# Masks built on GpSimd, single score tiles issued in runs, and a rewritten order, in a one-core attention plus feed-forward kernel

## The chip, the cores and the metric

The kernel runs on one core of a Trainium2 chip. A core has five engines that run side by side and meet through semaphores: TensorE (PE in the profile; PEld is its weight load), VectorE (DVE), ScalarE (ACT), GpSimd (POOL) and SyncE (SP), which here issues most of the data transfers. The metric is the device time of one execution in microseconds; the kernel before takes 184.63 us as the median of three runs (184.52 to 184.64).

## The reference

Four batches, eight heads, 768 positions, head size 64. Heads marked in `is_retrieval` see all earlier positions; the others see the first 4 positions (the sinks) and the last 64. After the attention, the 512 columns of the heads go through a feed-forward layer with two up projections of 1024 columns, their maximum, and one down projection.

```python
scores = scale * np.matmul(q, k.transpose(0, 1, 3, 2))
full_mask   = causal                              # retrieval heads: 0, 2 and 6
stream_mask = causal & (is_sink | in_win)         # the other five heads
a = softmax(np.where(mask, scores, -1e9))
x = np.matmul(a, v) -> (batch*seq, heads*head_dim)
out = np.maximum(x @ w1, x @ w2) @ w_out
```

## The kernel before, in words

**Pieces of work.** A batch is cut into two halves of 384 query rows, written (b, hf). For each half the heads are taken in four pairs; at run time `head_order` finds which heads are full ones, and the pairs are "FF", "FS", "SS", "SS". A pair of a half goes through these steps: a load of q, k and v into `ld` (`load_half`, by SP); casts to bf16 into `qb` and `vb` (`cast_qk`, `cast_v`, any of DVE, ACT, POOL); a transpose on PE into a PSUM bank (`turn`, line 712); the copy back into `qk` (`unturn`); copies for the window heads (`mix_k`, `mix_v` into `kx`, `vx`). Then come the scores (`scores`, matmuls at line 893, on 64 rows each, two heads side by side), their exponentials (`exp`, ACT, line 912) into one of the `at` buffers, a multiplication with 0/1 masks (`mask`, DVE, line 931), the weighted sums (`weighted`, line 956), the division (`normalise`), and the transpose of x.

**Feed-forward.** The maximum is rewritten: max(x w1, x w2) = relu(x (w1 - w2)) + x w2. `prep_weights` makes `w12` = w1 - w2 in four column chunks (`sub`, DVE, line 1122), and `w2o` = w2 w_out out of transposes of w2 (line 1138) and matmuls (line 1156). `forward` then computes, for each half, eight blocks of x times `w12` (line 1177), the relu, and the output from both parts (line 1227), which is copied to `ot` and stored by SP (line 1244).

**Order.** Every step is an `Op` with estimated costs on the engines that could do it; `Order.run` walks through time, and by ranks (`RANK`), free PSUM banks, waits and margins gives each engine its list of instructions. PE has several lists (scores "S", weighted sums "W", feed-forward "F", turns "TQ" and so on) and takes the first list whose head can run. These are estimates used while the program is built; on the chip only the resulting order and its semaphores count. SP issues the loads in the order of `LOADS` and the ranks: q, k, the mask table and v of the first half, q and k of the second, w2, v of the second half, w1. The four pieces of w_out are loaded by POOL (line 616). Until 38 us of the plan, PE gets matmuls on a zero tile (`warmer`, line 471) where it has nothing else.

**Masks.** Identity and masks (1152 bf16 columns) are computed on the host and held in a table in DRAM. ACT issues the load of the identity (line 1558), SP the load of the other 1024 columns (`load_table`, line 595) as its third transfer. DVE turns four parts of them into 0/1 masks (`kept`, line 646). In the very first half the masks are instead added into the scores by matmuls (line 867).

**Score tiles.** `attend` makes one step out of two tiles of scores at a time (`TOGETHER`; in the first half one), each tile with two PSUM banks; six `at` buffers hold the exponentials (`NAT`).

**The end.** The last rows of the output are made in two parts of 256 columns; ACT copies each to `ot` and SP stores it. A check (`judge`, `say`) writes a verdict; every engine loads it (line 1569) and jumps (line 1572) over a second program, `tile_any_heads`, that is there for inputs with another set of heads and doesn't run here. The end of the program is a barrier of all engines.

Of the kernel before, what the change touches and what calls it, by code (L numbers as in the profile page):

```python
# [11 lines left out]
F32 = mybir.dt.float32  # L12
# [27 lines left out]
def one(p, hh, blocks):  # L40
# [96 lines left out]
class Order:  # L137
# [6 lines left out]
    def __init__(self, banks, dummy, dummies_until):  # L144
        self.ops, self.lists, self.n, self.shift = [], {}, 0, 0.0
        self.banks, self.freed = [None] * banks, [0.0] * banks
        self.at, self.dummy, self.dummies_until = {}, dummy, dummies_until
# [41 lines left out]

    def run(self, names, allowed):  # L190
# [11 lines left out]
        rings, served = {"SP": [], "POOL": []}, [0.0, 0]  # L202
# [16 lines left out]
        def begin(o, e, t):  # L219
            cost = o.costs[e]  # L220
# [53 lines left out]
        left = len(self.ops)  # L274
        while events:
# [25 lines left out]
            while again:  # L301
# [20 lines left out]
                for relaxed in (False, True):  # L322
                    chosen = None
                    for n in names:
# [10 lines left out]
                        if o.claims and self.place(o.claims, False, SPARE.get(n, 0)) is None:  # L335
                            continue
                        chosen = n, o
                        break
                    if chosen:
# [4 lines left out]
                        begin(o, "PE", t)  # L344
                        again = True
                        break
                else:
                    if t < self.dummies_until:
                        spot = self.place([("dummy", 1)], False)
                        last = 0.107 if t < COLD_UNTIL else 0.056  # L350
                        if spot and (t < COLD_UNTIL or used(t) < WARM_SHARE):
                            self.dummy(spot["dummy"][0])
                            done_pe.append((t, t + last, 1.0))
                        if spot:
                            free["PE"] = t + last
                            push(t + last, None)
# [7 lines left out]
REGISTERS = 4.4  # L364
TURNED_BY_PE = (0,)
# [3 lines left out]
    'cast': 3.05, 'vcast': 13.85, 'unturn': 4.05, 'mix_k': -0.7, 'mix_v': -14.35, 'exp': 4.1,  # L369
    'mask': -5.1, 'norm': -4.75, 'take_x': -8.75, 'turn': 8.65, 'w2b': 9.4, 'sub': -4.6, 'w2t':  # L370
    -8.95, 'wob': -4.45, 'w2o': -10.4, 'relu': -0.25, 'load': 10.7, 'out': -0.6, 'h2': 7.85,
    'table': -2.75, 'vload': -2.25,
# [5 lines left out]
NAT = 6  # L378
# [23 lines left out]
DMA_LATE = {'SP': 2.7, 'POOL': 3.2}  # L402
RING = 4224
SPLIT = ((0, 0),)
K_BY_ACT = False
K_LANDS = 7.6
# [4 lines left out]
RATE = {'first': 0.3, 'long': 0.34, 'v': 0.27, 'w': 0.36, 'wo': 0.37, 'cast': 0.22}  # L411
SPARE = {}
STEP = 2.4
FF_STEP = -2.1
S_AFTER = 2
PE_BEGINS = 1.0
# [3 lines left out]
MARGIN = {'W': 2.0, 'S': 0.8, 'F': 2.0, 'TQ': 0.8}  # L420
X_MARGIN = 1.5


def tile_three_full_heads(
    tc, q, k, v, w1, w2, wo, out, tab, table_dram, heads, rez, found, verdict, warm, early_k, lds
# [18 lines left out]
    NLD, NQB, NQK, NMIX, NAT, NX, NXT, NG, NOUT = 3, 4, 8, 6, 6, 2, 4, 2, 4  # L444
# [33 lines left out]
    def copy(e, out, in_):  # L478
        if e == "ACT":
            nc.scalar.copy(out=out, in_=in_)  # L480
        else:
            eng[e].tensor_copy(out=out, in_=in_)  # L482

# [3 lines left out]
    def act(n):  # L487
        return 0.065 + n / 1200
# [17 lines left out]
    def load_half(b, hf, kinds=(0, 1, 2)):  # L506
# [33 lines left out]
        if (b, hf) == (0, 0) and 0 in kinds:  # L540
            order_.insert(2 if long else 2 * NT, (3, 0))
        for t, i in order_:
# [3 lines left out]
            if t == 3:  # L546
                bias_in.append(load_table(128, 1152))
            elif t < 2 and long:
# [45 lines left out]
    def load_table(lo, hi):  # L594
        return dma(0.262, lambda _: nc.sync.dma_start(
            out=tab[:, lo:hi], in_=table_dram.ap()[:, lo:hi]
        ), rate=0.4, parts=128, grain=85.0)

# [25 lines left out]
    for what in LOADS:  # L624
        kind, c = what[:2], int(what[2:]) if what[:1] == "w" else 0
        if what[0] in "AB":
            kinds = (2,) if what[1:] else (0, 1)
            load_half(0, "AB".index(what[0]), kinds)
            flow += loads[0, "AB".index(what[0]), kinds[-1]]
# [6 lines left out]
    registers = order.given(REGISTERS)  # L636

# [143 lines left out]
    def prepare(b, hf, p):  # L781
# [7 lines left out]
        else:  # L789
# [4 lines left out]
            for hh in range(2):  # L794
                for lo, hi in ((0, 1), (1, 2)) if (b, hf) in SPLIT else ((0, 2),):
# [3 lines left out]
                        tag=f"cast{b}.{hf}.{p}", rank=RANK["cast"], port=("DVE", "POOL"),  # L799
# [814 lines left out]
```

## Time and profile before

| | |
|---|---|
| median of three runs | 184.63 us (184.52 to 184.64) |
| the profiled execution, its own time | 184.92 us |
| its span, first to last instruction | 182.0 us |
| what lies around the span (difference) | 2.92 us |
| busy: PE, DVE, ACT, POOL | 94%, 53%, 72%, 23% of the span |
| granted TensorE clock | 0.998 |

The profile has a page and a trace. On the page are the busy times of the engines, the span in 40 slices, the transfers, the chain of work that ended last (followed back from the end), and groups of instructions by source line. The trace answers further questions: a timeline of one engine in a stretch of time, the busy time in chosen stretches, and all instructions of one source line with their times, also those that only an engine's sequencer runs (a name such as ACTq). In a timeline a row is: start in us, length in us, engine, line, operation, output<-input, shapes, count, and in brackets the idle time before it with what ended it. Matmuls of one row overlap, so the start of the next row tells how long a group took.

### The profile page before, as it was taken

What the parts mean: (1) busy time and instruction counts of PE and PEld (TensorE: products, weight loads), DVE (VectorE), ACT (ScalarE), POOL (GpSimd) and SP (SyncE); (2) the same over time, 40 slices, a digit from 0 to 9 for tenths busy, and PEclk for the clock granted to TensorE, in tenths of its full rate; (3) what the DMA queues carried; (4) which work ended last, traced back from release to release, by engine and by line L of the source; (5) the groups of instructions that cost most, each with busy time, mean ns of one, the idle gap of its engine ahead of it and who ended that gap; (6) DMA issues with size and microseconds to landing.
All of it is one profiled execution on the core that took longest, in us unless ns stands there. A gap on an engine that the chain in (4) does not pass through costs nothing.

```text
span 182.0 us, 4932 instructions
## 1 busy us (share of the span) xinstructions
PE 171.5 (94%) x1836; PEld 105.3 (58%) x1836; DVE 96.7 (53%) x283; ACT 131.6 (72%) x287; POOL 42.4 (23%) x77
## 2 busy tenths in 40 slices
PE   7599599989999999999999999999999999999991
PEld 7567486466647656565545565565466545545560
DVE  3356896599689984576247476656447500000000
ACT  3399794596899999999996984777797524525430
POOL 1000810100609489899580000000000000000000
PEclk9999999999999999999999999999999999999999
DMA  4999999999899999999999994160151052012022
GB/s 136 323 242 339 347 223 244 349 290 280 221 290 270 326 294 295 160 243 202 179 140 147 248 177 118 63 144 0 61 144 61 0 144 115 11 58 115 0 99 87
DMA packets 74930, 32.68 MB, mean 180 GB/s; under 512 B 54162, under 2 KB 71826, under 8 KB 74898
## 3 DMA queue, kind: packets, MB, share of 16 engines
q1 hardware_dynamic: 54848, 28.84, 62.4%
q0 software_dynamic: 19904, 3.41, 25.4%
q8 instruction: 16, 0.26, 0.6%
q14 instruction: 16, 0.13, 0.2%
q10 hardware_dynamic: 146, 0.03, 0.1%
HBM read 25.46 MB, written 6.29 MB: 174 GB/s over the span
## 4 chain that ended last, share of the span: by engine, by line
PE 64%; SPq 11%; DMA 9%; DVE 5%; ACT 4%; issue 2%; POOL 2%; POOLq 0%; DVEq 0%; ACTq 0%
PE ps L1227 30%; PE ps L1177 20%; DMA ld<-in_v_dram 6%; PE ps L956 6%; PE ps L893 6%; SPq L523 5%; SPq L608 3%; DMA ld<-in_q_dram 3%; DVE w L1122 2%; SPq L513 2%; PE ps L712 2%; ACT at L912 2%; ACT qk L480 1%; POOL qb L482 1%; DVE at L931 1%
## 5 line engine op out<-in xcount | busy, mean ns | idle before, releaser
L912 ACT ACTIVATE at<-ps 128x512 bf16<-128x512 f32 (+2 forms) x134 | 65.1, 601 | 3.5 <-PE ps L893 1.9
L1227 PE MATMUL ps<-wob,g 128*128 128x512 bf16 (+1 forms) x200 | 46.8, 371 | 0.2 <-ACT at L912 0.2
L1177 PE MATMUL ps<-xt,w 128*128 128x384 bf16 x256 | 46.0, 326 | 0.9 <-DVE w L1122 0.7
L1177 PEld LDWEIGHTS <-w 128*128 128x128 bf16 x256 | 23.6, 97 | 15.9 <-issue 0.9
L931 DVE TENSOR_TENSOR at<-at,tab 128x1024 bf16<-128x1024 bf16 (+5 forms) x49 | 25.6, 538 | 13.3 <-ACT at L912 13.0
L1201 ACT ACTIVATE g<-ps 128x384 bf16<-128x384 f32 x56 | 27.5, 504 | 7.0 <-PE ps L1177 6.5
L1227 PEld LDWEIGHTS <-g 128*128 128x128 bf16 x200 | 18.2, 98 | 17.8 <-issue 0.4
L480 ACT COPY ot<-ps 128x512 f32<-128x512 f32 (+1 forms) x20 | 11.4, 572 | 22.8 <-PE ps L1227 22.6
L1227 PE MATMUL ps<-w2o,xt 128*128 128x512 bf16 (+1 forms) x100 | 24.8, 371 | 0.3 <-ACT qk L480 0.3
L956 PEld LDWEIGHTS <-at 128*128 128x128 bf16 x477 | 19.9, 97 | 7.3 <-issue 0.2
L983 DVE TENSOR_TENSOR x<-ps,rez 128x192 f32 x64 | 22.8, 356 | 1.8 <-DVE x L983 0.2
L956 PE MATMUL ps<-vb,at 128*128 128x65 bf16 x387 | 21.6, 193 | 0.0
L482 POOL CAST qb<-ld 128x384 bf16 x23 | 12.1, 561 | 35.6 <-DMA ld<-in_k_dram 35.6
L893 PE MATMUL ps<-qk 64*128 64x128 bf16 (+1 forms) x322 | 20.2, 230 | 0.0
L893 PEld LDWEIGHTS <-qk 64*128 64x128 bf16 x322 | 12.0, 94 | 11.2 <-issue 8.2
L1227 PEld LDWEIGHTS <-xt 128*128 128x128 bf16 x100 | 9.2, 98 | 9.0 <-issue 0.5
L712 PE MATMUL ps<-tab,qb 128*128 128x128 bf16 x144 | 10.4, 219 | 4.0 <-DVE qb L482 2.1
L480 ACT COPY qk<-ps 128x768 bf16<-128x768 bf16 x17 | 12.9, 816 | 0.6 <-PE ps L712 0.6
L480 ACT CAST qb<-ld 128x384 bf16 (+1 forms) x23 | 8.8, 453 | 6.1 <-DMA ld<-in_k_dram 3.7
L471 PE MATMUL ps<-warmer 128*128 128x128 bf16 x147 | 11.0, 236 | 1.1 <-POOL warmer L1552 1.1
L712 PEld LDWEIGHTS <-qb 128*128 128x128 bf16 x144 | 8.3, 98 | 5.0 <-ACT qb L480 2.3
L471 PEld LDWEIGHTS <-warmer 128*128 128x128 bf16 x147 | 9.8, 107 | 1.4 <-POOL warmer L1552 1.1
(62 smaller groups left out, 145.5 us busy)
## 6 DMA issues: line engine op xcount, KB each, us to landing
out_dram<-ot SPq DMA_DIRECT2D x23, 256.0 KB, 2.1
ld<-in_q_dram SPq DMA_DIRECT2D x6, 768.0 KB, 7.0
ld<-in_k_dram SPq DMA_DIRECT2D x6, 768.0 KB, 7.4
ld<-in_v_dram SPq DMA_DIRECT2D x18, 256.0 KB, 6.7
ld<-in_moe_w_dram SPq DMA_DIRECT2D x8, 512.0 KB, 8.2
wob<-in_moe_w_out_dram POOLq DMA_DIRECT2D x4, 256.0 KB, 8.1
ld<-in_q_dram POOLq DMA_DIRECT2D x8, 96.0 KB, 6.6
ld<-in_k_dram POOLq DMA_DIRECT2D x8, 96.0 KB, 6.7
```

The lines of the kernel that those rows point to most:

```text
L471: nc.tensor.matmul(banks[e][:, 0:128], lhsT=warm, rhs=warm, start=True, stop=True)
L480: nc.scalar.copy(out=out, in_=in_)
L482: eng[e].tensor_copy(out=out, in_=in_)
L712: nc.tensor.transpose(to[:, i], qbs[:, T["qb", n, hf] % NQB, t, i].rearrange("p h d -> p (h d)"), ident)
L893: nc.tensor.matmul(to.rearrange("p (i c) -> p i c", c=128), lhsT=lhsT, rhs=q_of(n, i, m)[rows], start=bk not in under, stop=True, skip_gro ...
L912: nc.scalar.activation(out=at[:, bk, 0:w], in_=bank(("ps", b, hf, t), part=bk)[:, 0:w], func=ACT.Exp, scale=scale,)
L931: eng[e].tensor_tensor(out=at, in0=at, in1=tbl, op=ALU.mult)
L956: nc.tensor.matmul(po[:, hh, i - NT * hf, :], lhsT=ats[:, T["at", b, hf, t] % NAT, bk, e * 128:(e + 1) * 128], rhs=rhs, start=first, stop= ...
L983: nc.vector.tensor_tensor(out=xs[:, (2 * b + hf) % NX, :, bass.ds(heads[2 * p + hh], 1), :], in0=po[:, hh, :, 0:D].unsqueeze(2), in1=z[:, ...
L1177: nc.tensor.matmul(bank(key)[:, 0:HALF], lhsT=w[:, kc, fc * 128:(fc + 1) * 128], rhs=xts[:, (2 * b + hf) % NXT, :, kc, :], start=(kc == 0) ...
L1201: nc.scalar.activation(out=g, in_=ph, func=ACT.Relu)
L1227: nc.tensor.matmul(bank(key)[:, cols], lhsT=lhsT, rhs=(w2o if kind == "x" else wob)[:, c, cols], start=(e == 0), stop=(e == len(steps) - 1),)
```

## The change

1. The masks and the identity are no longer loaded. DVE zeroes the table, and POOL writes it with eight `affine_select` instructions and two copies (`mask_table`). The planner is told that they are there at 6.5 us (`MASKS_MADE`). The built program has, on POOL, one library-reload instruction ahead of the first select.
2. Each tile of scores is a step of its own; `run_of_scores` lets PE begin with scores only if two (at the end of a half three) tiles can be issued one after the other, with their banks free. The planner charges for entering and leaving scores.
3. `at` has eight buffers in place of six; `ok` lies in `lds`, whose loads are over by then.
4. The two halves of the first batch have ranks of their own (`FRONT`, `rank_of`), all ranks, margins, biases and rates have new numbers, and `LOADS` has the weights in another order. So the order of instructions is new on each engine.
5. The last store is issued by ACT, which also makes the copy before it (`LAST_BY_ACT`).
6. `tile_any_heads`, which doesn't run, takes three tiles of scores per exponential: its part on ACT shrinks from 393 to 135 instructions; those of PE, DVE and POOL (9803, 3165, 256) stay.

```diff
-TOGETHER = (
-    [[0, 1], [2, 3], [4, 5], [6]], [[0, 1], [2, 3], [4, 5], [6, 7], [8, 9]],
-    [[0], [1], [2], [3], [4], [5]],
-)
...
+    def run_of_scores(self, first, t):
+        mine = self.lists["S"][first:]
+        mine = [o for o in mine if o.tag[1:3] == mine[0].tag[1:3]]
+        n = 1 if self.stuck or mine[0].tag[1:3] == (0, 0) else min(S_RUN, len(mine))
+        if len(mine) - n == 1 and not self.stuck:
+            n += S_REST
+        if any(o.left or o.ready > t + 1e-9 for o in mine[:n]):
+            return False
+        return sum(e is None for e in self.banks) >= 2 * n
...
-                    for n in names:
+                    for n in ("S", *names) if last == "S" else names:
...
+                        if n == "S" and last != "S" and not self.run_of_scores(at[n], t):
+                            continue
...
+                        extra = ENTER_S if n == "S" and last != "S" else LEAVE_S if last == "S" and n != "S" else 0.0
...
+MASKS_MADE = 6.5
-NAT = 6
+NAT = 8
-    'A', 'Av', 'B', 'w23', 'wo0', 'wo1', 'wo2', 'w20', 'wo3', 'w21', 'w11', 'w10', 'w12', 'w22',
+    'A', 'Av', 'B', 'wo1', 'w20', 'w21', 'wo0', 'wo2', 'w12', 'w10', 'w23', 'w22', 'wo3', 'w11',
     'w13', 'Bv',
-BIAS = {'DVE': 1, 'ACT': 0}
+BIAS = {'DVE': 2.5, 'ACT': 0}
+LAST_BY_ACT = True
+S_RUN = 2
+S_REST = 1
+ENTER_S = 0.1
+LEAVE_S = 0.11
-MARGIN = {'W': 2.0, 'S': 0.8, 'F': 2.0, 'TQ': 0.8}
+MARGIN = {'W': 0.3, 'S': 0.8, 'F': 2.0, 'TQ': 0}
+FRONT = (
+    {'mix_k': -2.8, 'mask': -4.7, 'unturn': -0.4, 'exp': -10.3, 'vcast': -3.0, 'cast': -3.8,
+    'norm': -0.3}, {'vcast': -1.7, 'unturn': -1.3, 'exp': 0.5, 'mask': -2.7, 'norm': 4.4,
+    'mix_k': 1.8, 'cast': -1.5},
+)
...
-        if (b, hf) == (0, 0) and 0 in kinds:
-            order_.insert(2 if long else 2 * NT, (3, 0))
-            if t == 3:
-                bias_in.append(load_table(128, 1152))
...
+    bias_in.append(order.given(MASKS_MADE))
...
+                ends = LAST_BY_ACT and (b, i) == (B - 1, 2 * NT - 1) and part == len(parts) - 1
+                    (nc.scalar if ends else nc.sync).dma_start(
+                        out=out[r0:r0 + 128, cols], in_=ots[:, number % NOUT, cols]
+                    )
...
+def mask_table(nc, bias, n_sink, window):
+    at = lambda i, n=1: bias[:, 128 * i:128 * (i + n)]
+    def put(i, n, base, by_key, by_query, fill=-1e30):
+        nc.gpsimd.affine_select(
+            out=at(i, n).rearrange("p (n c) -> p n c", c=128), in_=at(i, n).rearrange("p (n c) -> p n c", c=128),
+            pattern=[[0, n], [by_query, 128]], compare_op=ALU.is_ge, fill=fill, base=base,
+            channel_multiplier=by_key,
+        )
+    put(7, 1, 0, -1, 1)
+    put(0, 1, n_sink - 1, -1, 0)
+    put(1, 2, window - 129, 1, -1)
+    put(2, 1, -n_sink, 1, 0, 0.0)
+    put(3, 3, window - 1, 1, -1)
+    put(3, 1, -n_sink, 1, 0, 0.0)
+    put(3, 3, 0, -1, 1)
+    nc.gpsimd.tensor_copy(out=at(6)[0:64], in_=at(0)[0:64])
+    nc.gpsimd.tensor_copy(out=at(6)[64:128], in_=at(1)[64:128])
...
         nc.gpsimd.memset(warmer, 0.0)
+        nc.vector.memset(tab[:, 0:1152], 0.0)
+        nc.gpsimd.affine_select(
+            out=tab[:, 0:128], in_=tab[:, 0:128], pattern=[[1, 128]], compare_op=ALU.not_equal, fill=1.0,
+            base=0, channel_multiplier=-1,
+        )
+        mask_table(nc, tab[:, 128:1152], n_sink, window)
         found, count = head_order(nc, consts, is_retrieval, H)
-        nc.scalar.dma_start(out=tab[:, 0:128], in_=table_dram.ap()[:, 0:128])
```

More of the change, by code (lines that the diff above doesn't have):

```diff
@@ L1248, in forward @@
                 )
+                if ends:
+                    op({"ACT": 0.5}, store, [ev], data=0.000512 * width_ / 0.38, grain=85.0)
+                    continue
                 ot_free[number].append(
```

229 lines of the change are left out of this document (111 added, 118 removed).

## The prediction

> **What bounds the kernel now.** First I cut the span into three stretches (busy time of each engine in chosen stretches), at the first feed-forward matmul and at PE's last one. Columns: start:end, length, busy us (instructions) of PE, PEld, DVE, ACT, POOL, granted clock, DMA share, GB/s.
>
> ```profile
> span 182.0 us, 4932 instructions
> ```
> ```profile
> 0.00:38.86 38.86, 33.09 (x483) 24.68 (x483) 24.77 (x84) 26.95 (x57) 5.81 (x14) 1.00 1.07 279
> 38.86:178.10 139.24, 138.39 (x1354) 80.63 (x1354) 71.94 (x200) 104.33 (x231) 36.62 (x63) 1.00 0.86 155
> 178.10:182.00 3.90, 0.00 (x0) 0.00 (x0) 0.00 (x0) 0.35 (x1) 0.00 (x0) 0.92 0.23 73
> ```
>
> From 38.86 us on PE is full (idle 0.85 us) at the full clock: there the time is PE's work. Before it the DMA engines are full (share 1.07): there the time is the arrival of data. The tail is 3.90 us without matmuls. So the time is 38.86 + 139.24 + 3.90 us of span, and 2.92 us around it in the profiled execution (184.92), which lies 0.29 us above the median of 184.63.
>
> What releases the first feed-forward matmul stands in the timelines of PE and DVE:
>
> ```profile
> 38.86 3.42 PE L1177 MATMUL ps<-xt,w 128*128 128x384 bf16 x20 [0.67 <-DVE w L1122]
> ```
> ```profile
> 33.69 0.87 DVE L482 CAST vb<-ld 128x192 bf16 x3 [3.31 <-DMA ld<-in_v_dram]
> 34.48 0.49 DVE L482 COPY vx<-vb 64x204 bf16<-64x204 bf16 x2
> 34.99 0.35 DVE L482 CAST vb<-ld 128x192 bf16 x1
> 35.26 0.68 DVE L482 CAST w2o<-ps 128x512 bf16<-128x512 f32 x1
> 35.98 0.56 DVE L482 COPY vx<-vb 64x408 bf16<-64x408 bf16 x2
> 36.45 3.48 DVE L1122 TENSOR_TENSOR w<-ld 128x1024 bf16<-128x1024 f32 x3
> 42.40 0.18 DVE L973 RECIPROCAL rez<-ps 128x6 f32<-128x6 f32 x1
> ```
>
> DVE idles 3.31 us until v of the second half lands, then works without a gap; two of the chunk differences (1.16 us each) end at 38.77, and PE starts 0.09 us later. So the first stretch is: landing of that v (33.69) + 5.17 us.
>
> **The change, part by part.**
>
> *No mask table on SP's queue.* 256 KB ahead of v leave a full queue.
>
> ```profile
> tab<-mask_table SPq DMA_DIRECT2D x1, 256.0 KB, 7.3
> ```
> ```profile
> 16.00:22.00 6.00, 4.14 (x92) 3.91 (x90) 4.65 (x16) 4.37 (x9) 3.01 (x5) 1.00 1.10 345
> ```
>
> At 345 GB/s they take 0.262 MB / 345 = 0.76 us, and everything behind lands that much sooner, v of the second half at 32.93. The order of SP's loads behind is otherwise the same. On POOL one of the four w_out pieces now stands ahead of the casts of the second half, without a wait; before, all four came behind them at 20.18. Its bytes only trade places ahead of that v (landing by the sum unchanged); the second half's q and k, 0.5 MB at 345 GB/s = 1.5 us later, less 0.76, land 0.75 us later. I cost that at nothing, because PE still had 5.5 us of filler ahead of 38.86:
>
> ```profile
> 18.99 1.24 POOL L482 CAST qb<-ld 128x384 bf16 x2 [14.28 <-DMA ld<-in_k_dram]
> 20.18 3.17 POOL L616 DMA_DIRECT2D wob<-in_moe_w_out_dram  x4
> ```
> ```profile
> 6.60:38.86 32.26, 5.53 (x76) 4.36 (x73) 1.00 1.15 296
> ```
>
> DVE's new list between that landing and the first pair of differences: five casts (1.22 + 0.25), two copies 0.49, a difference 1.16, a reciprocal 0.18, two copies 0.56, a difference 1.16 = 5.0, against 5.08 before. The same; first stretch 38.86 - 0.76 = **38.10 us**. PE must be through by then: behind its last filler its new list has 32 matmuls of 512 columns, 16 transposes, 32 score matmuls (with two entries) and 51 weighted sums up to the first feed-forward matmul; at the rates of the score part below (0.056 us for 128 columns, 0.031 a sum) these are 7.1 + 0.9 + 1.3 + 1.6 = 10.9 us. It is in time if that filler ends by 27.2.
>
> *Masks on POOL.* No row shows a select. POOL's casts give a line: (0.561 - 0.394)/192 = 0.87 ns a column and 0.227 us a start.
>
> ```profile
> L482 POOL CAST qb<-ld 128x384 bf16 x23 | 12.1, 561 | 35.6 <-DMA ld<-in_k_dram 35.6
> L482 POOL CAST vb<-ld 128x192 bf16 x20 | 7.1, 394 | 10.7 <-DMA ld<-in_v_dram 10.6
> L1560 ACT ACT_TABLE_LOAD x1 | 1.3, 1283 | 1.8 <-PEq L1595 1.8
> ```
> ```profile
> 8.55 0.87 DVE L482 CAST qb<-ld 128x192 bf16 x3 [1.32 <-DMA ld<-in_k_dram]
> 9.34 0.62 DVE L646 TENSOR_SCALAR tab<-tab 128x128 bf16<-128x128 bf16 x4
> ```
>
> Eight selects over 1664 columns and two copies of 128 come to 3.9 us, so begun at 1.5 us they are done at 5.4. POOL idles until 19 us, so it costs nothing there. But the change adds a wait: DVE's four mask steps (0.62 us) now stand ahead of its four casts of k and wait for POOL; behind them wait the casts, then PE's turns. They may begin at 8.55 - 0.62 = 7.9 at the latest, 2.5 us after my 5.4. The open price is the library reload ahead of the first select. From below it is 0 (it could already be there); the nearest row, ACT's table load, has 1.28; both fit into 2.5. The far row, PE's fetch of code over the jump (3.96, quoted below), would make k 1.4 us late. I take no cost, by the nearest row.
>
> The Trainium skill (GPSIMD Engine Reference, Instruction dispatch) states about 6 us for the first call into a freshly loaded kernel on GpSimd. By that the k casts are 3.5 us late, and the sum below would be 182.9 to 185.7. No row here shows such a load.
>
> *Runs of scores.* Counted in the order of instructions, PE enters scores 36 times before and 33 after, 25 and 22 behind the first feed-forward matmul. A row of the timeline starts where the last one's work has gone through:
>
> ```profile
> 57.30 0.53 PE L956 MATMUL ps<-vb,at 128*128 128x65 bf16 x12
> 57.67 0.83 PE L712 MATMUL ps<-tab,qb 128*128 128x128 bf16 x12
> 58.34 0.32 PE L956 MATMUL ps<-vb,at 128*128 128x65 bf16 x5
> ```
> ```profile
> 135.67 0.34 PE L956 MATMUL ps<-vb,at 128*128 128x65 bf16 x6
> 135.94 0.23 PE L893 MATMUL ps<-qk 64*128 64x128 bf16 x2
> 136.50 0.33 PE L956 MATMUL ps<-vb,at 128*128 128x65 bf16 x5
> ```
>
> Twelve weighted sums take 0.37 us, so six take 0.185; ahead of scores they take 0.27: entering costs 0.085. Twelve turns take 0.67, or 0.056 for 128 columns; sixteen score matmuls, two side by side, should take 0.447 and take 0.56: leaving costs 0.11. Three runs fewer at 0.2 are **0.6 us**. All other matmuls have the same number and shape. Eight `at` buffers, the moved `ok` and the program that doesn't run add no instruction to the path. ACT gets six casts and loses seven relus (to DVE, 52% busy in that stretch) and two casts of v: about even.
>
> *The last store.* These rows are of the sequencers, from the lines of the store, the verdict, the jump and the final barrier:
>
> ```profile
> 178.08 0.37 ACT L480 COPY ot<-ps 128x256 f32<-128x256 f32 x1 [0.89 <-PE ps L1227]
> ```
> ```profile
> L1244 SPq DMA_DIRECT2D out_dram<-ot x1: 864/864/864, 178.5 to 178.5; - x1
> DMA to landing us min/median/max: 2.2/2.2/2.2
> ```
> ```profile
> L1569 ACTq TENSOR_LOAD <-verdict x1: 296/296/296, 178.1 to 178.1; - x1
> L1569 SPq TENSOR_LOAD <-verdict x1: 546/546/546, 179.4 to 179.4; - x1
> ```
> ```profile
> L1572 POOLq EVENT_SEMAPHORE  x4: 17/43/43, 157.7 to 157.9; - x4
> L1572 POOLq COMPARE_BRANCH  x1: 45/45/45, 154.9 to 154.9; - x1
> L1572 PEldq COMPARE_BRANCH  x1: 3960/3960/3960, 176.6 to 176.6; - x1
> L1572 ACTq COMPARE_BRANCH  x1: 50/50/50, 178.4 to 178.4; - x1
> L1572 ACTq EVENT_SEMAPHORE  x1: 17/17/17, 181.0 to 181.0; - x1
> ```
> ```profile
> L1609 SPq DRAIN  x2: 7/10/13, 181.1 to 181.2; - x2
> L1609 POOLq EVENT_SEMAPHORE  x2: 17/17/17, 181.2 to 181.3; - x2
> ```
>
> The barrier at 181.2 has two late comers. SP issues 0.86 us, loads the verdict 0.55, jumps, works through its waits, and is done at 181.2; ACT jumps at 178.4 and is there at 181.0, 2.55 us for 393 skipped instructions. SP now ends earlier with issuing and only waits for the store to land, about 178.5 + 2.2 = 180.7; PE's jump ends at 180.56; the barrier could come at 180.85: -0.35 us. But ACT now does issue (to about 179.0; half of SP's 0.86 taken, its queue being empty), load (0.3) and jump behind its copy. With a jump of 2.55 us it arrives at 181.85: +0.65. Its skip is 135 instructions now; POOL's 256 took 2.8 us, SP's one 0.2. Between these I take the short jump, as 135 is the nearer to one, by little.
>
> The Trainium skill (Runtime: NRT & Kernel Launch, Instruction fetch mechanics) says that a jump stalls for a fetch when its target lies outside the two blocks of 256 instructions at hand. By it ACT's old target (some 840 instructions in, jump at 447) is outside and the new one (576) inside: -0.35. POOL's 2.8 us over 256 instructions doesn't bear it out plainly.
>
> *Sum.* 38.10 + (139.24 - 0.6) + (3.90 - 0.35) = 180.3 of span, 183.2 with the 2.92 around it, and 0.29 less against the median: **182.9 us**, 1.7 us faster.
>
> **The rivals.**
>
> *The masks come late (slower).* If POOL's load takes L, k is L - 2.5 us late at DVE, and all of the first half behind it. PE has only 0.7 us of idle and filler left just ahead of 38.86, so at worst L - 3.2 arrives at the end: it eats the whole gain at L = 4.9 (masks at 10.3), and slower begins there. At L = 8 it is 182.9 + 4.8 = 187.7 if all is passed on; PE's filler could swallow half: 185.3. I take 186. For it speaks that the reload has no row and that DVE idled only 1.32 us before k; against it POOL's and ACT's known starts.
>
> *The front gains nothing.* The w_out piece taken early delays the second half's casts by 0.75 us, or ACT, busy 27 of 39 us, ends late: first matmul at 38.9. 182.9 + 0.76 = 183.7.
>
> *ACT's jump stays long.* The tail is +0.65 in place of -0.35: 183.9.
>
> *The runs wait.* A run of scores needs four free banks; PE idles in the full stretch. Idle now 0.85 us; tripled: 182.9 + 1.7 = 184.6, no change. Against it: feed-forward matmuls stand ready through that stretch.
>
> **How the numbers follow.** Forecast 0.46; late masks 0.23; no gain in front 0.12; long jump 0.13; waiting runs 0.06. Forecast alone: 182.2 to 183.5. Low end 181.9: PE's front could also use the earlier data. High end 186.2, past most of the late masks. 0.2% (0.37 us) is what a measurement tells from no change: faster, the forecast, the front, the jump and a small part of the late masks, 0.72; same 0.05; slower, the rest, 0.23.
>
> **What would show it.** Last v of the front landing near 32.9 and the first feed-forward matmul at 38.1; DVE's mask steps beginning before 7.9; 22 score runs behind; PE's idle behind 38 under 1.2 us; ACT past its jump before 180 and the barrier at PE's end + 2.8. I am wrong if DVE stands waiting for POOL after 8.5 us, or ACT comes last to the barrier.

## The result, and the profile after

The changed kernel takes **185.84 us** (median of six runs, 185.32 to 186.47) against 184.64 for the kernel before on the same chip: the ratio is 1.0071, with a 95% interval of 1.0044 to 1.0099. It is 1.2 us slower; 182.9 was forecast. The execution profiled took 185.75 us, with a span of 184.1. In all that follows, medians are of all executions of a kernel, while ratios leave out those that took over 1.5% more than its fastest.

The stretches of the changed kernel, cut as in the prediction (columns as there):

```profile
0.00:38.90 38.90, 36.23 (x511) 27.49 (x513) 25.10 (x85) 28.74 (x60) 9.64 (x25) 1.00 1.07 281
38.90:179.45 140.55, 137.51 (x1333) 81.02 (x1348) 74.50 (x203) 105.05 (x229) 33.76 (x59) 1.00 0.88 150
179.45:184.10 4.65, 0.00 (x0) 0.00 (x0) 0.00 (x0) 0.37 (x1) 0.00 (x0) 1.00 0.19 62
```

| part, us | before | forecast | after | off the forecast |
|---|---|---|---|---|
| up to the first feed-forward matmul | 38.86 | 38.10 | 38.90 | +0.80 |
| to the last copy | 139.24 | 138.64 | 140.55 | +1.91 |
| tail | 3.90 | 3.55 | 4.65 | +1.10 |
| around the span | 2.92 | 2.92 | 1.65 | -1.27 |
| profiled execution | 184.92 | 183.2 | 185.75 | +2.54 |

All four terms were off. Some matmul records are missing in this trace (1333 where there should be about 1350), so part of the 3 us by which PE's busy time falls short of 140.55 is not idle time. I therefore reckoned PE's waits from the starts of all matmuls: the time from one start to the next, less that of the columns, less 0.2 us for each run of scores, with missing ones put back. By that, PE's waits behind the first feed-forward matmul are **1.4 us before and 3.6 after**; entering and leaving scores costs 5.2 us (25 runs) before and 4.6 (22 runs) after; what is left, 132.6 and 132.4 us, is the matmuls themselves. The level hangs on what is taken for a matmul's own time (with the median of each shape both waits come out about 1 us higher), the rise of some 2 us does not.

**The masks.** POOL and DVE in the changed kernel's timeline:

```profile
1.73 0.29 POOL L1590 TENSOR_SCALAR_AFFINE_SELECT tab<-tab 128x128 bf16<-128x128 bf16 x1 [0.60 <-DVE tab L1589]
1.98 2.69 POOL L1540 TENSOR_SCALAR_AFFINE_SELECT tab<-tab 128x128 bf16<-128x128 bf16 x7
4.61 0.28 POOL L1552 COPY tab<-tab 64x128 bf16<-64x128 bf16 x1
4.95 0.29 POOL L1553 COPY tab<-tab 64x128 bf16<-64x128 bf16 x1
```

POOL waited 0.60 us for DVE's zeroes, not for its own code, and is done at 5.24. DVE's mask steps start at 6.42, ahead of k.

**The front.** PE and DVE ahead of the first feed-forward matmul (line 1194):

```profile
24.80 1.68 PE L499 MATMUL ps<-warmer 128*128 128x128 bf16 x27
...
26.90 1.12 PE L499 MATMUL ps<-warmer 128*128 128x128 bf16 x17
27.96 0.49 PE L920 MATMUL ps<-qk 64*128 64x384 bf16 x3
...
28.66 1.07 PE L1155 MATMUL ps<-tab,w2b 128*128 128x128 bf16 x16
29.56 5.34 PE L1173 MATMUL ps<-wob,w2t 128*128 128x512 bf16 x23
...
35.62 1.24 PE L983 MATMUL ps<-vb,at 128*128 128x65 bf16 x35
...
37.17 1.89 PE L1173 MATMUL ps<-wob,w2t 128*128 128x512 bf16 x7
38.90 4.06 PE L1194 MATMUL ps<-xt,w 128*128 128x384 bf16 x24
```
```profile
31.93 1.39 DVE L510 CAST vb<-ld 128x192 bf16 x5 [0.79 <-DMA ld<-in_v_dram]
33.24 0.48 DVE L510 COPY vx<-vb 64x204 bf16<-64x204 bf16 x2
33.75 1.23 DVE L1139 TENSOR_TENSOR w<-ld 128x1024 bf16<-128x1024 f32 x1
36.80 0.20 DVE L1000 RECIPROCAL rez<-ps 128x6 f32<-128x6 f32 x1 [1.82 <-PE ps L983]
```

v of the second half lands at 31.93, a full us earlier than forecast. But PE is busy without a gap from the last filler (line 499, to 27.96) to 38.90, and DVE's reciprocal, which stands in its list between the chunk differences, waits 1.82 us for PE's weighted sums. The late part is now PE's list.

**The full stretch.** Two stretches of 6 us (start:end, length, PE's busy time), the kernel before and then the changed one, and what stands behind the second:

```profile
50.00:56.00 6.00, 5.78 (x63) 1.00 1.16 285
98.00:104.00 6.00, 6.00 (x64) 1.00 1.74 229
```
```profile
50.00:56.00 6.00, 5.27 (x60) 1.00 0.97 239
98.00:104.00 6.00, 5.41 (x59) 1.00 1.63 196
```
```profile
99.62 1.05 ACT L508 COPY vx<-vb 64x340 bf16<-64x340 bf16 x3
100.69 0.49 ACT L1218 ACTIVATE g<-ps 128x384 bf16<-128x384 f32 x1
```
```profile
100.44 0.30 PE L983 MATMUL ps<-vb,at 128*128 128x65 bf16 x4
101.23 0.97 PE L1194 MATMUL ps<-xt,w 128*128 128x384 bf16 x5 [0.50 <-ACT g L1218]
```

PE waits for the bank that a relu on ACT frees, and ACT has three copies of v ahead of that relu. The new waits are short like this one (0.1 to 0.7 us), for a relu, a copy or a mask that comes late, and nearly all lie between 53 and 108 us.

**The tail.** Rows of the sequencers, at the store (1263), the jump (1613) and the final barrier (1650):

```profile
L1263 ACTq DMA_DIRECT2D out_dram<-ot x1: 384/384/384, 179.9 to 179.9; - x1
```
```profile
L1613 PEldq COMPARE_BRANCH  x1: 3613/3613/3613, 177.9 to 177.9; - x1
L1613 SPq COMPARE_BRANCH  x1: 53/53/53, 179.6 to 179.6; - x1
L1613 ACTq COMPARE_BRANCH  x1: 54/54/54, 180.6 to 180.6; - x1
L1613 PEldq EVENT_SEMAPHORE  x1: 51/51/51, 181.6 to 181.6; - x1
L1613 ACTq EVENT_SEMAPHORE  x1: 17/17/17, 183.1 to 183.1; - x1
```

ACT jumps at 180.6 and is through at 183.1: 2.5 us, although 135 instructions are skipped now and not 393. It is the last at the barrier.

### The profile page after: what moved, and what is told of

It is laid out like the page before. It is cut to its first block, busy times and chain, and to the rows that moved or that the text cites. A ratio compares the mean times of both kernels' runs of the same rounds, so it can differ in the third digit from the quotient of the medians.

```text
span 184.1 us, 4968 instructions
## 1 busy us (share of the span) xinstructions
PE 173.7 (94%) x1842; PEld 108.5 (59%) x1861; DVE 99.6 (54%) x287; ACT 134.2 (73%) x287; POOL 43.4 (24%) x84
## 4 chain that ended last, share of the span: by engine, by line
PE 69%; DVE 10%; ACT 6%; DMA 5%; SPq 4%; issue 3%; DVEq 0%; ACTq 0%
PE ps L1244 27%; PE ps L1194 20%; PE ps L983 7%; PE ps L920 7%; DMA ld<-in_k_dram 5%; PE ps L1173 4%; SPq L556 3%; DVE x L1010 3%; PE ps L738 2%; ACT at L939 2%; DVE kx L510 2%; PE ps L499 2%; DVE at L958 1%; SPq L546 1%; DVE vx L510 1%
## 5 line engine op out<-in xcount | busy, mean ns | idle before, releaser
L939 ACT ACTIVATE at<-ps 128x512 bf16<-128x512 f32 (+2 forms) x134 | 63.8, 590 | 4.5 <-PE ps L920 4.2
L1244 PE MATMUL ps<-wob,g 128*128 128x512 bf16 (+1 forms) x192 | 45.3, 370 | 0.5 <-issue 0.3
L958 DVE TENSOR_TENSOR at<-at,tab 128x1024 bf16<-128x1024 bf16 (+5 forms) x49 | 24.7, 521 | 13.6 <-ACT at L939 13.1
L1218 ACT ACTIVATE g<-ps 128x384 bf16<-128x384 f32 x49 | 24.4, 505 | 5.3 <-PE ps L1194 5.1
L1244 PE MATMUL ps<-w2o,xt 128*128 128x512 bf16 (+1 forms) x91 | 24.2, 370 | 0.5
L983 PEld LDWEIGHTS <-at 128*128 128x128 bf16 x477 | 19.5, 97 | 8.1 <-DVE at L958 1.1
L510 POOL CAST qb<-ld 128x384 bf16 x18 | 9.5, 566 | 34.8 <-DMA ld<-in_k_dram 23.9
L499 PE MATMUL ps<-warmer 128*128 128x128 bf16 x172 | 14.4, 248 | 1.2 <-POOL warmer L1588 1.2
L508 ACT CAST qb<-ld 128x384 bf16 (+1 forms) x29 | 11.4, 471 | 4.0 <-DMA ld<-in_k_dram 2.3
L499 PEld LDWEIGHTS <-warmer 128*128 128x128 bf16 x172 | 12.6, 114 | 1.6 <-POOL warmer L1588 1.2
L1220 DVE TENSOR_SCALAR g<-ps 128x384 bf16<-128x384 f32 x15 | 8.2, 554 | 6.6 <-ACT at L939 3.1
```

Of the source, the lines that this page charges most:

```text
L499: nc.tensor.matmul(banks[e][:, 0:128], lhsT=warm, rhs=warm, start=True, stop=True)
L939: nc.scalar.activation(out=at[:, bk, 0:w], in_=bank(("ps", b, hf, t), part=bk)[:, 0:w], func=ACT.Exp, scale=scale,)
L958: eng[e].tensor_tensor(out=at, in0=at, in1=tbl, op=ALU.mult)
L983: nc.tensor.matmul(po[:, hh, i - NT * hf, :], lhsT=ats[:, T["at", b, hf, t] % NAT, bk, e * 128:(e + 1) * 128], rhs=rhs, start=first, stop= ...
L1218: nc.scalar.activation(out=g, in_=ph, func=ACT.Relu)
L1244: nc.tensor.matmul(bank(key)[:, cols], lhsT=lhsT, rhs=(w2o if kind == "x" else wob)[:, c, cols], start=(e == 0), stop=(e == len(steps) - 1),)
```

## The experiments

The traces list the transfers that bring an engine's code; the changed kernel's rows for the two code queues are (packets, MB, share):

```profile
q8 instruction: 16, 0.26, 0.6%
q14 instruction: 15, 0.12, 0.3%
```

0.26 MB in 16 is 16 KB each, and their times go with PE's progress; 0.12 MB in 15 is 8 KB each. From one of the 16 KB packets to the next the trace has some 250 instructions of PE and its weight load, which fits 64 bytes an instruction: blocks of 256 for PE and of 128 for the rest. This became the key to the tail. In the experiments on it the work that runs keeps its order on every engine, except for the store where the diff says so. Ratios are to the kernel before, with the 95% interval.

**The tail: store and fallback, one at a time.**

```diff
-LAST_BY_ACT = True
+LAST_BY_ACT = False
```

> The changed kernel with one thing undone: the last store is issued by SP again, everything else in the same order on every engine. Theory 'ACT's jump': in the changed kernel ACT starts its jump 1.15 us after its last copy begins (issue of the store 0.38, load of the verdict 0.30 ahead of it) and needs 2.5 us for it, so it comes last to the barrier. With the store on SP, ACT should again start its jump 0.35 us after the copy's start and arrive 2.9 us after it, SP 3.1 us after it: the barrier moves from 3.85 to 3.1 us behind the last copy's start, and the time falls by 0.7 us, from 185.84 to 185.1. Rival 'landing': the tail is set by the landing of the last store, whoever issues it: 185.8, no change. PE's end stays where it is, 179.3 us, in both.

Measured: 184.88 us, ratio 1.0021 (0.9994 to 1.0049), where the changed kernel had 1.0071. PE's end is at 179.4, the barrier completes 3.2 us behind the last copy's start: as the theory of the jump expected.

```diff
-nc.sync.dma_start(out=out[r0:r0 + 128, cols], ...)
+(nc.scalar if ends else nc.sync).dma_start(out=out[r0:r0 + 128, cols], ...)
```

> The kernel before with one thing done: the last store is issued by ACT, everything else in the same order. Theory 'ACT's jump stays long': ACT loads the verdict and jumps only behind its issue, as in the changed kernel 1.15 us behind the start of its last copy, and arrives 3.65 us behind it: 178.08 + 3.65 = 181.73 against the barrier at 181.2, so about 0.6 us more, 185.2. Rival of the prediction, 'SP was the late one': 0.35 us less, 184.3.

Measured: 184.83 against 184.38 us, ratio 1.0015 (0.9989 to 1.0041), not to be told from no change. ACT comes last to the barrier, at 182.3, as expected and even later; but the time around the span falls from 2.4 to 1.9 us in the median. Where the rest of the 0.6 us went was open here; f1 below suggests an answer.

The fallback programs of the two kernels exchanged:

> The changed kernel with the old fallback program (393 instructions on ACT instead of 135), which isn't run. Theory 'the jump's time doesn't hang on the number of skipped instructions': ACT's jump takes 2.5 us again, span 184.1, time 185.8. Rival 'the jump grows with the length': ACT's jump was 2.55 us with 393 in the kernel before and should then be as long here and the changed kernel's shorter; it isn't shorter there, so a growth is expected only if the two jumps differ here. For the time around the span (2.92 us before, 1.65 after): if it comes with the size of the program, it is 2.9 here and the time 187.1; if it comes with the mask table that is no longer a constant in memory, it stays at 1.65 and the time at 185.8.

Measured: 186.21 us, ratio 1.0083 (1.0051 to 1.0114); ACT's jump 2.55 us, around the span 1.67. Neither changes with the longer program.

> The kernel before with the new, shorter fallback program, which isn't run. SP comes last to the barrier there, so a shorter jump of ACT would gain nothing: span 182.0. For the time around the span: if it comes with the size of the program, it falls to 1.65 here and the time to 183.4; if with the mask table, it stays at 2.9 and the time at 184.6.

Measured: 184.42 us, ratio 1.0001 (0.9978 to 1.0024), around the span 2.9, unchanged again. But ACT's jump, of 137 instructions, is short here:

```profile
L1577 ACTq COMPARE_BRANCH  x1: 50/50/50, 178.4 to 178.4; - x1
L1577 ACTq EVENT_SEMAPHORE  x1: 17/17/17, 179.5 to 179.5; - x1
```

So a jump over the same length takes 1.1 us here and 2.5 in the changed kernel. Counted in the compiled programs, it stands at ACT's instruction 447 here and at 441 there. If a block's edge lies between these two, the target is one block on here and two blocks on there. The trace's packets speak for that edge: here an 8 KB block is asked for at 177.8, as ACT comes to its jump, and the jump is through 1.2 us after that packet's end; in the changed kernel none is asked for before 181.6, 1.0 us into the jump. The test is to shorten the jump where it stands (six score tiles per exponential in the fallback):

```diff
-                if i % 3 < 2:
+                if i % 6 < 5:
```

> The changed kernel with ACT's part of the fallback program, which isn't run, cut from 135 to 71 instructions; the work that runs is in the same order. The traces show that ACT's code comes in pieces of 8 KB (128 instructions of 64 bytes, PE's in 16 KB). Theory 'blocks of 128': ACT's jump is short only if its target lies in the block fetched last ahead of it. In the changed kernel the jump stands at instruction 441 and its target 136 further on, two blocks on; in the kernel before with the 137-instruction fallback it stood at 447, one block further, and took 1.1 us. With 71 the target is one block on, the jump takes under 1.2 us in place of 2.5, ACT is at the barrier by 181.8, SP is last at 182.0 and the time falls by about 1.1 us, to 184.7. Rival 'a jump of ACT takes 2.5 us unless something else is under way': it arrives at 183.1 again, 185.8.

```profile
L1613 ACTq COMPARE_BRANCH  x1: 54/54/54, 181.2 to 181.2; - x1
L1613 ACTq EVENT_SEMAPHORE  x1: 17/17/17, 181.7 to 181.7; - x1
L1613 PEldq EVENT_SEMAPHORE  x1: 51/51/51, 182.5 to 182.5; - x1
```

Measured: 184.59 us, ratio 0.9992 (0.9968 to 1.0015). The jump takes 0.5 us, with no packet asked for during it; PE and then SP come last now. That agrees with blocks of 128.

**The front: the fillers.**

```diff
-                            self.dummy(spot["dummy"][0])
+                            if t < 22:
+                                self.dummy(spot["dummy"][0])
```

> The changed kernel with the last 46 filler matmuls of the first stretch left out (2, 27 and 17 in a row, at 24.2 to 28.0 us), everything else in the same order. Theory 'PE's list is what holds the front': the scores behind the last filler run stood ready, so the products of w2 and w_out start up to 1.1 us earlier, the weighted sums and the reciprocal that the chunk differences wait behind too, and the first feed-forward matmul starts at about 38.0 instead of 38.9; time 185.0. Rival 'PE would wait there anyway', for ACT's exponentials and DVE's cast of w2: the start stays at 38.9, 185.8.

PE and DVE of this run:

```profile
27.72 1.05 PE L1156 MATMUL ps<-tab,w2b 128*128 128x128 bf16 x16
...
38.05 2.28 PE L1195 MATMUL ps<-xt,w 128*128 128x384 bf16 x13
```
```profile
35.95 0.20 DVE L1001 RECIPROCAL rez<-ps 128x6 f32<-128x6 f32 x1 [0.96 <-PE ps L984]
```

Measured: 184.32 us, ratio 0.9976 (0.9960 to 0.9992). Everything behind the fillers comes 0.85 to 0.95 us sooner and the first feed-forward matmul starts at 38.05: the fillers held the front. The time falls by more than that, because the stretch behind is shorter too (139.9 us to the last copy). The fillers may not be for nothing: without them 12 of 36 executions in orders of the changed kernel (4 here, the rest in e10 and e11) had a mean granted clock of 0.991 or less and took 1 to 2.5 us longer, with them 2 of 48 (the changed kernel, e1, e2, e7, e9). In the kernel before, 29 of 134 had such a clock with the fillers, and their median was the same.

> The kernel before without its last 22 filler matmuls of the first stretch, everything else in the same order. Theory of the prediction 'there the landing of v sets the front': PE waited 0.67 us for DVE's differences ahead of its first feed-forward matmul, so it stays at 38.9 and the time at 184.5. Rival 'fillers hold the front in both kernels, and the table's 0.76 us were worth nothing': it comes to 38.1 here too and the time to 183.7.

Measured: 183.26 us, ratio 0.9925 (0.9900 to 0.9950). Neither theory: the time fell by 1.4 us, but not by an earlier first feed-forward matmul (39.3, in a front with a clock of 0.96; f2 below shows the same order at full clock). The time around the span fell to 1.7 us.

```diff
-table_dram = nc.inline_tensor(table, name="mask_table")
+mask_table(nc, tab[:, 128:1152], n_sink, window)
```

> The kernel before with the masks and the identity made by POOL and no mask table in memory; all numbers of the order as before, from which the order follows anew. Theory of the prediction 'the table's 0.76 us on the full queue set the front': v of the second half lands at about 32.9 and the first feed-forward matmul starts at 38.1, which gives 183.7. Rival 'PE's own list sets the front as soon as data come sooner': it starts at 38.9, 184.4. For the time around the span, 2.4 us in the median for the kernel before and 1.65 in the changed one: if the table's constant makes it, it is 1.65 here and the time lower by another 0.8.

Measured: 184.45 us, ratio 0.9970 (0.9935 to 1.0005). The execution profiled took 187.49 us, with v landing as late as 34.16; the first feed-forward matmul starts at 39.03, 4.87 us behind it, so there the landing sets the front and not PE's list. Where it stands in the others remains open. Around the span 1.9 us.

**The full stretch: margins and numbers.**

```diff
-MARGIN = {'W': 0.3, 'S': 0.8, 'F': 2.0, 'TQ': 0}
+MARGIN = {'W': 2.0, 'S': 0.8, 'F': 2.0, 'TQ': 0.8}
-X_MARGIN = 0.4
+X_MARGIN = 1.5
```

> The changed kernel with the planner's margins of the kernel before (a weighted sum, a turn by TensorE and a turned x are planned 2.0, 0.8 and 1.5 us behind their input instead of 0.3, 0 and 0.4); the whole order of the work follows from that anew. Theory 'too little slack': the waits of PE behind the first feed-forward matmul, some 2 us more than before in the changed kernel, come from matmuls placed right behind their inputs; with the old margins they fall to about 1 us more or none, PE's end moves from 179.3 to 177.5 to 178.3, and the time from 185.84 to about 184.3. Rival 'other numbers of the order': the waits stay at 2 us more and the time at 185.5 to 186.

Measured: 183.92 us, ratio 0.9966 (0.9943 to 0.9989), faster than both kernels. PE's waits fall from 3.6 to 2.3 us and the stretch to 139.5. ACT has 454 instructions ahead of its jump in this order, behind the block's edge, and its jump takes 0.5 us; the tail is 3.9 us from PE's end. The first feed-forward matmul stays at 39.0.

> The kernel before with the changed kernel's margins (0.3, 0 and 0.4 us instead of 2.0, 0.8 and 1.5); the order follows anew from the old planner. Theory 'too little slack': PE's waits behind its first feed-forward matmul rise by about 1 us, from 1.4 to 2.4, the time to 185.4. Rival 'the margins matter only together with the other new numbers': waits as before, 184.5.

Measured: 188.31 us, ratio 1.0188 (1.0143 to 1.0233). PE's waits rise to 2.8 us, somewhat more than expected; but 2 us more are lost at the very end, where PE had come through its jump at 182.4 and still signs on to the barrier only at 185.7:

```profile
L1572 PEldq EVENT_SEMAPHORE  x1: 51/51/51, 182.4 to 182.4; - x1
```
```profile
L1609 PEldq DRAIN  x2: 8/8/8, 185.7 to 186.0; - x2
```

Between the two the trace has one 16 KB block of code, from 183.1 to 184.1.

**The place of PE's code.** Three kernels with more transposes in the fallback, which doesn't run, so that PE's last instructions lie elsewhere in a block of 256:

```diff
+    for _ in range(24):
+        nc.tensor.transpose(pad[:, 0:128], ident, ident)
```

> The kernel before with 48 more TensorE instructions in the fallback program, which isn't run: the work that runs and its order are untouched, only PE's code behind the jump lies 48 instructions further on (13553 in all instead of 13505; 241 instead of 193 over a multiple of 256). Theory 'code position': PE's code comes in blocks of 16 KB (256 instructions), and in the kernel before its last few instructions lie over a block's edge, so that the end waits for one more block (1.0 to 1.4 us, asked for 0.7 us behind PE's landing from the jump): the time around the span is 2.4 to 2.9 us there and 1.65 in the changed kernel (242 over). Padded, it falls to 1.65 and the time from 184.6 to 183.6 to 183.9. Rival 'the inline table or the order of the changed kernel makes the time around': nothing changes, 184.6.

Measured: 183.32 against 184.85 us, ratio **0.9925** (0.9894 to 0.9956); around the span 1.77 us in the median against 2.85, as the theory of the code's place expected. 48 instructions that never run make the kernel before 1.4 us faster. The trace of the kernel before has the block that is waited for: it is asked for at 181.3, 0.7 us behind PE's landing, and comes to 182.7, past the end of the span.

> The kernel before without its last 22 fillers, and with 44 more TensorE instructions in the fallback program, so that PE's code ends at 13505 again as in the kernel before. Theory 'code position': the gain of leaving the fillers out there (184.6 to 183.3) came for the most part from the code's place; with the place restored the time around the span is above 2 us again and the time 184.0 to 184.3. Rival 'the fillers themselves': it stays at 183.3.

Measured: 183.86 us, ratio 0.9954 (0.9926 to 0.9983), around the span 2.55. Between the two theories: the place gives back about 0.5 us, the rest of that gain came from the span. This profile has e12's order at full clock, and it answers what e12 left open: v lands at 33.27, the first feed-forward matmul starts 5.16 us later, and PE waits for DVE's difference, as the prediction read the kernel before.

```profile
38.43 1.80 PE L1178 MATMUL ps<-xt,w 128*128 128x384 bf16 x10 [0.74 <-DVE w L1123]
```

> The kernel before with the changed kernel's margins, and 49 more TensorE instructions in the fallback program (13560 in all, 248 over a multiple of 256, instead of 13511 and 199). Theory 'code position': of the 3.7 us that the new margins cost there, 2.1 to 2.5 were PE's wait for a code block inside the span, between its landing at 182.4 and its arrival at the barrier at 185.7; they go, and what is left is the order: PE's end 180.0, span 184.0, time 185.7, 1.1 us over the kernel before. Rival: 188.3 again.

```profile
L1575 PEldq EVENT_SEMAPHORE  x1: 51/51/51, 182.1 to 182.1; - x1
```
```profile
L1612 PEldq DRAIN  x2: 8/8/8, 182.2 to 183.2; - x2
```

Measured: 186.35 us, ratio 1.0114 (1.0062 to 1.0167). PE's 3.3 us between its landing and the barrier are 0.1 now. Against f1, the kernel before padded in the same way, the new margins cost 3.0 us.

**What the old numbers are worth, and a kernel that beats both.**

> The changed kernel with all numbers of the order (ranks, order of the loads, biases, rates, steps, margins; no separate ranks for the first batch) as in the kernel before, and ACT's part of the fallback at 71 instructions; masks by POOL, runs of scores, eight tiles of weights and the store by ACT as changed. Theory 'the new numbers make PE's waits': the waits behind the first feed-forward matmul fall from 3.6 to about 1.4 us, the runs of scores keep their 0.6, so that this stretch takes 138.4 us instead of 140.35 and the time is about 183.5. Rival 'the new rules make them' (runs of scores wait for four free banks, whatever the numbers): waits of 3 us or more, time 185.

Measured: 183.67 us, ratio 0.9944 (0.9915 to 0.9973). The waits are 2.6 us: one us less than with the new numbers, one more than expected. The first feed-forward matmul starts at 37.7. With the old order of loads the front goes as forecast: v lands 0.85 us sooner than before, and the feed-forward starts 4.84 us behind it, PE waiting for DVE's difference:

```profile
32.84 1.39 DVE L506 CAST vb<-ld 128x192 bf16 x5 [3.06 <-DMA ld<-in_v_dram]
37.68 2.77 PE L1190 MATMUL ps<-xt,w 128*128 128x384 bf16 x16 [0.26 <-DVE w L1135]
```

> The same as the kernel with the old numbers of the order (rules, masks and store as changed, ACT's fallback at 71 instructions), without its last 54 fillers of the first stretch. Behind the first feed-forward matmul the order is the same as there, so this is also a second look at PE's waits in it. If data arriving late made the 1.6 us of waits at 70 to 72 us there, they come out differently here; if the order made them, the same, near 2.6 us in all. Front: if fillers were in the way, the first feed-forward matmul comes before 37.7 and the time below 183.3; if not, both stay, 37.7 and 183.7. For the kernel before the time is 184.6 to 184.9.

Measured: **182.99 us** against 184.95, ratio 0.9898 (0.9869 to 0.9927), the best kernel here. The first feed-forward matmul starts at 37.8, the waits are 2.5 us and in the same places. As the front hardly moved, this doesn't tell the order from late data; at 70 to 72 us the profile names an exponential and a copy on ACT, not a load, as what PE waits for. Two combinations came out thus:

> The changed kernel's own order, without the last 46 filler matmuls of the first stretch and with ACT's part of the fallback cut to 71 instructions. If front and tail are separate causes: first feed-forward matmul at 38.05, PE's end at 177.8, ACT at the barrier 1.6 us behind its last copy, span 181.8, time 183.4. Rival 'the tail's gain is eaten by another late comer': PE itself, which jumped 3.6 to 4.0 us after its last instruction but one and arrived 2.5 us behind the last copy, holds the barrier; span 181.8 to 182.2, time 183.4 to 183.8.

Measured: 183.22 us, ratio 0.9911 (0.9881 to 0.9941); first feed-forward matmul at 37.9, PE's end at 177.05, span 180.9. Front and tail add up, and the waits shrink too, to 2.4, though this stretch has the changed kernel's order and margins. Part of what is gone shows in the timelines: first the changed kernel, where PE waits 0.28 us for one of DVE's copies of k (`kx`), then this one, where it doesn't.

```profile
51.99 3.21 POOL L510 CAST qb<-ld 128x384 bf16 x6 [4.46 <-DMA ld<-in_k_dram]
53.96 1.87 DVE L510 COPY kx<-qk 64x128 bf16<-64x128 bf16 x5
55.30 0.23 PE L920 MATMUL ps<-qk,kx 64*128 64x128 bf16 x2 [0.28 <-DVE kx L510]
```
```profile
54.12 3.54 POOL L511 CAST qb<-ld 128x384 bf16 x6 [5.46 <-DMA ld<-in_k_dram]
52.29 0.84 DVE L511 COPY kx<-qk 64x128 bf16<-64x128 bf16 x5
```

The five copies take 1.87 us while POOL casts, and 0.84 when they are through before POOL starts. With nothing but the fillers and the long jump undone, the span is 180.9, where 180.3 was forecast.

> The changed kernel with the old margins and, in that order, the last 43 filler matmuls of the first stretch left out. If the two causes add up (fillers 0.85 us in the start of the first feed-forward matmul, margins 1.0 us in the stretch behind it and, with ACT's jump short in that order, 1 us in the tail), the first feed-forward matmul starts at about 38.1, PE ends at 177.4 and the time is 183.0, faster than the kernel before. Rival 'the front is held by something else in that order': start at 39.0, time 183.9 as with the margins alone.

Measured: 184.50 us, ratio 0.9988 (0.9953 to 1.0024). The profiled execution has 183.56 with a start at 38.4 and PE's end at 177.8, near what was expected, but six of twelve ran at a clock of 0.987 to 0.991 and took 184.8 to 186.0. The stretch takes 139.5 us to the last copy, as with the old margins alone (e2, 139.5) or the fillers out alone (139.9 in e5, 139.4 in e11): there the two gains don't add.

## Why the prediction was wrong, point by point

- **First stretch, 38.10: wrong at the step "PE must be through by then".** The bytes of the table were gone and v landed a full us sooner than the forecast's 32.93. (The table gave what was reckoned: f4, which has the old order of loads, lands v at 32.84. The rest comes with the new numbers; one of the w_out pieces, which I let trade places for nothing, is issued at 6.15 there and at 19.5 with its fellows in f4.) The condition that I wrote down, "in time if that filler ends by 27.2", failed: it ended at 27.96, and with the 10.9 us of PE's list behind it that gives 38.9, the start measured. I left the filler's end unchecked. e5 shows that the fillers were the cause: without them the start is 38.05, near the 38.10 forecast, though by another way, as PE's list still ends it there. Where PE does wait for DVE (f2, f4), the chain of the forecast holds.
- **Masks: right.** Done at 5.24 (forecast 5.4), DVE's mask steps at 6.42, and no wait for code shows ahead of POOL's first select. The Trainium skill's 6 us for a first call (GPSIMD Engine Reference, Instruction dispatch) are not seen here: the select starts at 1.73.
- **Runs of scores, -0.6: the count was right** (22), and at unchanged 0.2 us each that gain is there. The step that failed is "(139.24 - 0.6)", which put the rest of the new order at nothing: PE's waits in the full stretch rose by 2.2 us. That is about the size of the rival that I gave 0.06, but by another mechanism: most are waits for a late relu, copy or mask and not of a run of scores for banks. The steps to "add no instruction to the path" looked at what runs, not at how much slack is left between a producer and PE.
  What makes the waits is shown in part only. Going back to the old margins removes 1.3 of the 2.2 (e2), to all the old numbers 1.0 (f4, f5), and the new margins alone add 1.4 to the kernel before (e13). But leaving out the fillers removes 1.2 with order and margins kept (e11), and both together no more (e10), so e2 doesn't prove the margins; e13 and f3 speak for them more plainly. One way to lose time is seen in e11: DVE's copies are slow when they meet POOL's casts, which start when data land. And one order differs from profile to profile: to the last copy the kernel before's takes 138.4 to 140.3 us (e8, the kernel itself, e4, f1), the changed one's 140.6 to 140.9 (the kernel itself, e1, e7, e9). The rise is clear, its size is not; some 1 us of waits remains with the new rules under old numbers, and its cause is not settled.
- **Tail, -0.35: wrong at "I take the short jump".** The rival "ACT's jump stays long" held: the tail is 0.75 us longer than before (+0.65 there). The Trainium skill's rule (Runtime: NRT & Kernel Launch, Instruction fetch mechanics), a window of two blocks, has the right form, but its 256 instructions a block are PE's here; ACT's blocks have 128. With that and an edge between ACT's instructions 441 and 447, which was read from the jumps themselves and from the packets of code, 441 to 577 is out of the window, 447 to 584 inside (1.1 us), and 441 to 513 inside (0.5 us); all three were measured.
- **Around the span, 2.92 taken over unchanged: wrong by 1.27, in the kernel's favour.** f1 to f3 show that it depends on where PE's last instructions lie in a block. In the kernel before they lie 193 over a multiple of 256, and its end waits for one more block of code; in the changed one 242 over. A later barrier hides that wait as well (e4: 2.4 to 1.9); how much of the 1.27 is the place and how much the longer tail was not separated.
- **The rivals were set as alternatives.** The times of three of them came together: front without gain, long jump, waiting runs. Only the jump came as it was described: the front was held by fillers and not by late casts, and the waits were mostly not those of runs. Their prices by the forecast, 0.76, 1.0 and 1.7 us, sum to 186.4, and with the 1.27 taken off to 185.1. The sizes were fair, for two of them by luck; what failed was to let only one happen at a time.

## What to carry to other kernels

Where an order is planned with slack, look at the slack: put into the kernel before, matmuls placed 0.3 us behind their planned input cost 1.4 us in waits (e13), while three switches fewer gain 0.6. Fillers meant to keep a clock up are work like any other once data come sooner; check what stands behind the last one. And before comparing two builds to a per cent, compare where their code ends: a program whose last instructions, or whose jump's target, fall over a block's edge pays 1 to 3 us that no line of the kernel shows.

## What the runs showed of the hardware that I had not expected

- Code comes in blocks of 16 KB for PE and 8 KB for the other engines. ACT's jump took 2.5 to 3.0 us with its target two or more blocks on, 1.1 into a next block asked for just ahead of the jump (e8), 0.5 into a next block fetched earlier (e2, e9, e10, e11), and 0.2 within its own block (f4, f5).
- PE asks for the block behind its landing 0.6 to 1.2 us after it, and the block takes 0.9 to 1.4 us. If its last instructions lie in that block, the end waits. PE's code length over a multiple of 256 and the cost: 190, around the span 1.9 us (e3); 193, 2.4 to 2.9 (1.9 in e4, where the store by ACT makes the barrier later); 199, 3.3 us inside the span (e13); 148 to 158 and 212 to 248, none (1.6 to 1.8).
- DVE's copies and multiplications from one bf16 tile to another are slower while POOL casts: in the changed kernel 0.46 us in place of 0.25 for a copy of 128x320, 0.73 in place of 0.55 for a mask step of 128x768. The division out of PSUM (128x192) takes 0.36 us in both cases.
- 48 instructions that never run changed the time by 0.75% (f1), as much as the whole change under study.
